# A decode kernel at full DMA: last V chunk in two transfers, output tiles ahead, half of the norm first, two weight blocks on ScalarE's queue

## Chip, core and metric

One core of one Trainium2 chip. The metric is the device time of one execution in microseconds (us), the median of several; the profile is one execution with the hardware profiler. "PE" is the matmul engine, "DVE" VectorE, "ACT" ScalarE, "POOL" GpSimd, "SP" SyncE, which issues most transfers.

## The reference, cut to what matters

One token for each of 8 sequences goes through two passes of the same pair of layers: grouped-query attention over a cache of 4096 keys and values, then a small mixer MLP.

```
def _A_ref(x, k_cache, v_cache, wq, wo):        # x: (8, 1, 448); caches: (8, 8, 4096, 256), bf16
    q = x @ wq                                  # 16 heads of 256
    p = softmax(q k^T / 16); o = p v
    return o @ wo
def _B_ref(x, w1, w2, w3, w4):
    ...                                         # with one token, the shifted mixer adds nothing
    return x1 + gelu(layernorm(x1) @ w3) @ w4
x = x + A(layernorm(x)); x = x + B(layernorm(x)); x = x + A(layernorm(x)); x = x + B(layernorm(x))
```

K and V are far larger than the on-chip memory, and the second attention needs the result of the first, so most of the caches is read twice: the trace counts 446.8 MB of reads, nearly all in chunks of 1 MB. The on-chip memory has 128 rows, called partitions; a "half block" below is a transfer that fills 64 of them.

## The kernel before

Fifteen places of 1 MB take chunks of K and V in turn; SP issues a load as soon as a place is free. While they stream, each K chunk is transposed on DVE and multiplied on PE, each V chunk multiplied on PE. Layer B of the last four sequences follows the last V chunk, so it is alone at the end. The parts that the change touches (cuts are marked `...`):

```
def load_split(t, src, cols):                   # wq (cols 4096) and w3 (cols 1792), 448 rows
    for fc in range(3):                         # three full blocks of 128 rows
        nc.sync.dma_start(t[:, fc * cols : (fc + 1) * cols], src[fc * 128 : fc * 128 + 128, :])
    nc.sync.dma_start(t[0:64, 3 * cols :], src[384:448, 0 : cols // 2])     # last 64 rows: left half
    nc.sync.dma_start(t[64:128, 3 * cols :], src[384:448, cols // 2 :])     # and right half below it
...
def norm(x, nb, twice):                         # twice: layernorm of a layernorm, two scales
    ...
    nc.vector.tensor_scalar(ve[:, 0], var, 0.0, EPS, ALU.max, ALU.add)
    if twice:
        nc.vector.tensor_scalar(ve[:, 1], var, 0.0, EPS * EPS / (1 + EPS), ALU.max, ALU.add)
    rs = room("rs", (1, 2), 560)[:, 0]
    nc.gpsimd.tensor_tensor(rs[...0:n], ve[...0:n], nhalf[...], ALU.pow)     # one power for both scales
    nc.vector.tensor_tensor(xc, x, bc(mv[:, 0]), ALU.subtract)
    ...                                         # xb, input of the next matmuls, uses rs[:, n - 1] only
    nc.vector.tensor_tensor(xc, xc, bc(rs[:, 0]), ALU.mult)                  # the other scale: residual
    nc.vector.tensor_add(x, x, xc)
...
    nc.sync.dma_start(dst[:], src)              # every K or V chunk, in emit_loads
...
    # after the last chunk:
    nc.vector.tensor_add(xs, xs, st["y"])       # residual of the attention
    nc.vector.tensor_copy(ident2, identb[:])    # identity for adding x in the output matmuls
    nc.vector.memset(o_row, 0.0)                # clear the output tile
    run(mlp_hidden(MID, Bn - MID))              # norm, @ w3, gelu
    ...                                         # @ w4, add x, four small stores
```

The softmax here doesn't subtract the row's maximum and nothing guards it: scores larger than these inputs give would overflow.

## Time and profile before

| what | value |
|---|---|
| three runs | 1115.7, 1116.61, 1117.74 us |
| profiled execution, span | 1110.0 us |
| DMA busy, mean rate over the span | full until the last slice, 404 GB/s |
| PE, DVE busy | 60%, 53% |
| last V chunk lands | 1095.86 us, 14.14 us before the end |

The lines that carry this stand in the prediction. The profiled span is shorter than the timed median because the time includes start and end around the instructions, some 1.8 us in this run (1111.84 against 1110.0), and because runs of one kernel differ by several us.

### The profile page before, as it was taken

The numbers are of one execution on the slowest core, as the hardware profiler recorded it, in microseconds if no ns is written. First come the engines' busy times: TensorE is split into PE (matmuls) and PEld (weight loads), VectorE is DVE, ScalarE is ACT, GpSimd is POOL, SyncE is SP. The second block draws the span as 40 slices with busy tenths as digits, with TensorE's granted clock in tenths as the row PEclk, the third lists the DMA queues.
The fourth block names the chain that finished last, engine by engine and source line by source line (L and its number), as shares of the span: only waits on it lengthen the run. The fifth ranks groups of instructions, "written<-read, shape, count | busy, mean of one in ns | idle before, by whom it ended". The sixth has DMA issues, their size and how long they took to land. (4 is left out here: it accounts for less than half of the span.)

```text
span 1110.0 us, 33816 instructions
## 1 busy us (share of the span) xinstructions
PE 666.6 (60%) x15606; PEld 463.1 (42%) x15606; DVE 592.6 (53%) x1010; ACT 124.6 (11%) x362; POOL 15.6 (1%) x25
## 2 busy tenths in 40 slices
PE   3135568556854578446674467844676467767775
PEld 2123345334542355324452245523454345535454
DVE  5145554646365555556465464655638463675362
ACT  0001001110110111100020000200111101111010
POOL 0000000000000000000000000000000000000000
PEclk9999999655575555555575555555557555565565
DMA  9999999999999999999999999999999999999994
GB/s 357 384 421 419 418 389 421 420 409 403 417 418 421 395 407 418 419 421 397 396 422 420 420 399 409 420 420 415 404 418 420 415 407 416 419 417 396 409 416 166
DMA packets 65181, 448.96 MB, mean 404 GB/s; under 512 B 6920, under 2 KB 10896, under 8 KB 11408
## 3 DMA queue, kind: packets, MB, share of 16 engines
q1 hardware_dynamic: 65008, 446.80, 98.4%
q8 instruction: 122, 2.00, 0.7%
q14 instruction: 19, 0.16, 0.0%
q10 hardware_dynamic: 32, 0.00, 0.0%
HBM read 446.77 MB, written 0.01 MB: 403 GB/s over the span
## 5 line engine op out<-in xcount | busy, mean ns | idle before, releaser
L632 DVE STREAM_TRANSPOSE places<-places 128x1024 uint32<-128x1024 uint32 x400 | 469.4, 1219 | 277.8 <-DMA places<-in_A_k_cache_dram 275.3
L647 PE MATMUL sc<-places,qbd 128*8 128x128 bf16 (+1 forms) x7072 | 270.2, 306 | 292.6 <-DVE places L632 250.1
L647 PEld LDWEIGHTS <-qbd 128*8 128x8 bf16 x7072 | 171.1, 106 | 366.6 <-issue 181.5
L702 PE MATMUL o<-places,ptw 128*8 128x256 bf16 x3968 | 246.1, 392 | 102.8 <-DMA places<-in_A_v_cache_dram 86.9
L656 ACT ACTIVATE p_n<-sc 128x256 bf16<-128x256 f32 x128 | 95.9, 749 | 833.6 <-PE sc L647 833.6
L702 PEld LDWEIGHTS <-ptw 128*8 128x8 bf16 x3968 | 114.2, 111 | 150.1 <-issue 108.1
L337 PEld LDWEIGHTS <-wo_sb 128*128 128x128 bf16 x1280 | 38.7, 103 | 22.9 <-issue 22.7
L284 PEld LDWEIGHTS <-wq_sb 128*128 128x128 bf16 x1152 | 35.6, 104 | 25.8 <-issue 19.0
L310 DVE TENSOR_SCALAR qbd<-misc,quad 128x64 bf16<-128x64 f32 x64 | 13.7, 277 | 52.7 <-PE misc L304 52.7
L284 PE MATMUL misc<-xb,wq_sb 128*128 128x1 bf16 x1024 | 34.4, 166 | 4.7 <-ACT ptw L690 2.8
L337 PE MATMUL misc<-OT,wo_sb 128*128 128x1 bf16 x1024 | 34.8, 165 | 2.3 <-issue 2.3
L656 ACT ACTIVATION_READ_ACCUMULATOR p_n<-sc 128x1 f32 x128 | 34.2, 267 | 0.0
L441 PEld LDWEIGHTS misc<-R,o_sb 128*128 128x128 f32 x124 | 27.3, 305 | 10.2 <-issue 9.4
L690 ACT CAST ptw<-misc 128x128 bf16<-128x128 f32 x64 | 17.5, 273 | 118.4 <-PE misc L683 63.6
L441 PE MATMUL misc<-R,o_sb 128*128 128x8 f32 x124 | 30.0, 352 | 0.2
L241 POOL TENSOR_TENSOR t<-t,nhalf 128x2 f32<-128x2 f32 (+2 forms) x18 | 13.3, 739 | 1080.4 <-DVE t L248 1080.4
L674 DVE STREAM_TRANSPOSE places<-store 128x512 uint32<-128x512 uint32 x32 | 20.1, 684 | 11.5 <-PE sc L647 11.5
L355 PEld LDWEIGHTS <-w_sb 128*128 128x128 bf16 x560 | 17.2, 105 | 10.4 <-issue 9.2
L410 PE MATMUL misc<-zm,one 128*128 128x8 f32 (+1 forms) x66 | 18.6, 356 | 4.3 <-ACT ptw L690 2.4
L355 PE MATMUL misc<-xb,w_sb 128*128 128x1 bf16 (+1 forms) x560 | 18.6, 166 | 4.0 <-DVE xb L261 2.9
L410 PEld LDWEIGHTS misc<-zm,one 128*128 128x128 f32 x66 | 15.7, 296 | 10.9 <-issue 3.7
L667 DVE STREAM_TRANSPOSE store<-places 128x512 uint32<-128x512 uint32 x32 | 20.0, 693 | 0.5
(93 smaller groups left out, 228.2 us busy)
## 6 DMA issues: line engine op xcount, KB each, us to landing
places<-in_A_v_cache_dram SPq DMA_DIRECT2D x216, 1024.0 KB, 11.0
places<-in_A_k_cache_dram SPq DMA_DIRECT2D x200, 1024.0 KB, 11.7
wo_sb<-in_A_wo_dram SPq DMA_DIRECT2D x1, 3584.0 KB, 25.3
wq_sb<-in_A_wq_dram SPq DMA_DIRECT2D x3, 1024.0 KB, 6.9
w_sb<-in_B_w_dram SPq DMA_DIRECT2D x1, 1568.0 KB, 15.5
w_sb<-in_B_w_dram SPq DMA_DIRECT2D x3, 448.0 KB, 25.2
wq_sb<-in_A_wq_dram SPq DMA_DIRECT2D x2, 256.0 KB, 10.2
w_sb<-in_B_w_dram SPq DMA_DIRECT2D x2, 112.0 KB
```

The lines of the kernel that those rows point to most:

```text
L284: nc.tensor.matmul(q_ps[:, j * Hq + h, :], w, xbs(nb)[:, xi, :], start=(fc == 0), stop=(fc == 3),)
L337: nc.tensor.matmul(y_ps[:, fc, :], w[:, i, at : at + 128], rhs(i), start=start, stop=stop, skip_group_check=open is not None,)
L355: nc.tensor.matmul(h_ps[:, c * nb : c * nb + nb], w, xbs(nb)[:, xi, :], start=(fc == 0), stop=(fc == 3),)
L410: nc.tensor.matmul(z_ps, ones, zm[:], start=True, stop=True)
L441: nc.tensor.matmul(ot_ps[:, j], o_sb[:].rearrange("p (i j) -> p j i", j=2)[:, j], R[:], start=True, stop=True)
L632: nc.vector.transpose(w, w)
L647: nc.tensor.matmul(sc[32 * k : 32 * k + 8, 128 * x : 128 * (x + nx)], qbd[:, ep, gp].rearrange("p a h -> p (a h)"), v, start=(n == 0), sto ...
L656: nc.scalar.activation(p_sb[:, :, :, 2 * u : 2 * u + 2].rearrange("p t i x -> p x t i"), sc[:, 256 * u : 256 * u + 256].rearrange("p (x t ...
L667: nc.vector.transpose(store[n][:].bitcast(U32), slot[:].bitcast(U32)[:, 512 * n : 512 * n + 512])
L674: nc.vector.transpose(slot[:].bitcast(U32)[:, 512 * n : 512 * n + 512], store[n][:].bitcast(U32))
L690: nc.scalar.copy(ptw[:, :, :, 6:8], pt_ps.rearrange("p t k (a h) -> p a (t k) h", a=4),)
L702: nc.tensor.matmul(o_ps[32 * q : 32 * q + 8, 0:256], ptz[:, at : at + 8], v[:, y * Dh : (y + 1) * Dh], start=(begin and y < 4), stop=(y >= ...
```

## The change

Its intent: shorten the chain of dependent work after the last landing, and let the two half blocks of wq and w3 be issued by two engines. The diff, cut to its core:

```
-        nc.sync.dma_start(t[64:128, 3 * cols :], src[384:448, cols // 2 :])
+        nc.scalar.dma_start(t[64:128, 3 * cols :], src[384:448, cols // 2 :])
...
+        def power(k0, k1): nc.gpsimd.tensor_tensor(rs[:, k0:k1] ..., ve[:, k0:k1] ..., ALU.pow)
         if twice:
             nc.vector.tensor_scalar(ve[:, 1], var, ...)
+            if nb > 1:
+                power(1, 2)                      # the half that xb needs
+        nc.vector.tensor_scalar(ve[:, 0], var, ...)
+        power(0, 2 if twice and nb == 1 else 1)
...
-            nc.sync.dma_start(dst[:], src)
+            if loads:
+                nc.sync.dma_start(dst[:], src)
+            else:                                # the last chunk
+                for y in range(2):
+                    nc.sync.dma_start(dst[:, 8 * Dh * y : 8 * Dh * (y + 1)], src[:, 8 * Dh * y : ...])
...
     for idx, it in enumerate(items):
+        if idx == len(items) - 2:
+            ...                                  # ident2 copy and o_row memset, moved here from the end
```

More of the change, by code (lines that the diff above doesn't have):

```diff
@@ L236, in norm, with power @@
         n = 2 if twice else 1
-        nc.vector.tensor_scalar(ve[:, 0], var, 0.0, EPS, ALU.max, ALU.add)
+        rs = room("rs", (1, 2), 560)[:, 0]
+        def power(k0, k1):
+            nc.gpsimd.tensor_tensor(
+                rs[:, k0:k1].rearrange("p n b -> p (n b)"),
+                ve[:, k0:k1].rearrange("p n b -> p (n b)"),
+                nhalf[:].to_broadcast([128, (k1 - k0) * nb]),
+                ALU.pow,
+            )
         if twice:
             nc.vector.tensor_scalar(ve[:, 1], var, 0.0, EPS * EPS / (1 + EPS), ALU.max, ALU.add)
-        rs = room("rs", (1, 2), 560)[:, 0]
-        nc.gpsimd.tensor_tensor(
-            rs[:, 0:n].rearrange("p n b -> p (n b)"),
-            ve[:, 0:n].rearrange("p n b -> p (n b)"),
-            nhalf[:].to_broadcast([128, n * nb]),
-            ALU.pow,
-        )
+            if nb > 1:
+                power(1, 2)
+        nc.vector.tensor_scalar(ve[:, 0], var, 0.0, EPS, ALU.max, ALU.add)
+        power(0, 2 if twice and nb == 1 else 1)
         xc = room("xc", (1, 4), 576)[:, 0]
@@ L623, in emit_loads @@
                 src = rows.rearrange("(p x y) d -> x p (y d)", x=4, y=16)[c]
-            nc.sync.dma_start(dst[:], src)
+            if loads:
+                nc.sync.dma_start(dst[:], src)
+            else:
+                for y in range(2):
+                    nc.sync.dma_start(
+                        dst[:, 8 * Dh * y : 8 * Dh * (y + 1)], src[:, 8 * Dh * y : 8 * Dh * (y + 1)]
+                    )
             n += 1
@@ L775 @@
     for idx, it in enumerate(items):
+        if idx == len(items) - 2:
+            end = [slots[p] for p in places[:2]]
+            ident2 = end[0][:, 0:256].bitcast(FP32)
+            nc.vector.tensor_copy(ident2, identb[:])
+            W = D // 4
+            o_row = store[0][:, 0:W]
+            nc.vector.memset(o_row, 0.0)
         n, kv, c = it
@@ L882 @@
         step(10 * len(items))
-    end = [slots[p] for p in places[:2]]
     xs = xT[:, :, MID:]
     nc.vector.tensor_add(xs, xs, st["y"])
-    ident2 = end[0][:, 0:256].bitcast(FP32)
-    nc.vector.tensor_copy(ident2, identb[:])
-    W = D // 4
-    o_row = store[0][:, 0:W]
-    nc.vector.memset(o_row, 0.0)
     run(mlp_hidden(MID, Bn - MID))
```

## The prediction

> **What bounds the kernel now.** I read the page first. Its slice rows say the transfers bound the kernel from the first slice to the last but one: in these 40 slices of 27.75 us a digit is the busy share of the 16 DMA engines in tenths, and below it stands what they moved.
>
> ```profile
> PE   3135568556854578446674467844676467767775
> DVE  5145554646365555556465464655638463675362
> DMA  9999999999999999999999999999999999999994
> GB/s 357 384 421 419 418 389 421 420 409 403 417 418 421 395 407 418 419 421 397 396 422 420 420 399 409 420 420 415 404 418 420 415 407 416 419 417 396 409 416 166
> ```
>
> No compute engine is full, DMA is full until the last slice. So 446.8 MB of reads set the time, and only two stretches can be shortened: the **head**, where the transfers start, and the **tail**, from the last landing to the end. Everything between is bytes that the change leaves alone. I then read the chain of waits that ended last (start, duration, what), cut to the tail:
>
> ```profile
> 1075.93 19.93 DMA places<-in_A_v_cache_dram
> 1095.86 0.05 issue
> 1095.91 1.03 PE store L716 x32
> ...
> 1097.82 0.17 DVE xT L887
> 1097.99 0.14 DVE places L889
> 1098.12 0.02 issue
> 1098.14 0.15 DVE store L892
> ...
> 1100.37 0.02 POOLq L241
> 1100.39 0.07 issue
> 1100.45 1.68 POOLq L948
> 1102.14 0.02 issue
> 1102.16 0.18 DVE xb L261
> ```
>
> The last V chunk lands at 1095.86 and the span ends at 1110.0: 14.1 us of tail, one instruction after another. In it are the four things the change touches: 32 matmuls behind one landing (1.03 us), the two DVE set-up instructions L889 and L892 between the residual add L887 and the norm, and 1.68 us in which DVE waits for GpSimd's power. The same chain shows nothing of the head, so I asked for the DMA activity of the first 15 us and for windows there (last column GB/s, before it the DMA share):
>
> ```profile
> GB/s 0 0 0 0 19 175 87 175 284 393 415 415 481 393 371 437 415 481 393 393 481 415 459 371 415 459 426 306 262 240 219 240 295 262 306 371 393 415 415 437
> 7.00:10.00 3.00, 0.20 (x2) 0.10 (x1) 0.51 (x3) 0.00 (x0) 1.39 (x1) 1.00 1.01 426
> 10.00:13.00 3.00, 0.19 (x1) 0.10 (x1) 0.00 (x0) 0.00 (x0) 0.00 (x0) 1.00 1.05 268
> ```
>
> A slice of the first row is 0.375 us. There is a ramp up to about 3.4 us, then full rate, then a hole of some 3 us at about 10 to 13 us where the engines are busy (1.05) but move 268 GB/s: those are the two half blocks of wq, each of 64 partitions.
>
> **What the Trainium skill says.** "SBUF — State Buffer", section on the DMA port swizzle: partitions 0 to 63 reach only the eight even ports, 64 to 127 only the eight odd ones, so a 64-partition transfer gets half the bandwidth. The trace agrees: down to 219 to 262 GB/s in the hole, against 426 just before. "DMA: Bandwidth & Descriptors", section "Issuing engines are not separate DMA queues": transfers of ScalarE and SyncE run on the same 16 engines, and a second issuer saves issue time only. The trace before has no second issuer under load, so it cannot confirm this. "GPSIMD Engine Reference", section 3.1, gives about 2.6 cycles per element for a two-input operation. Our power is far dearer by the rows below, and the rows decide.
>
> **The change part by part.**
>
> *1. Last V chunk in two transfers (tail).* The transfers of 1 MB come every 1.0486 MB / 423 GB/s = 2.48 us (423 GB/s in the window 1080 to 1085 us). The first half should land about 1.2 us before the second. The instruction order with waits shows that the first 16 matmuls then wait for the first half's semaphore and matmul 17 for the second's. 16 of 32 matmuls move ahead of the last landing: 1.03 / 2 = **-0.51 us**. Cost: rows of 4 KB instead of 8 KB, and one more issue. SP issues the last V at 1075.93, 20 us before it lands, so the issue is hidden. In the packet records an 8 KB packet takes 309 ns and an uncontended 4 KB one 159 ns; an engine has 8 rows, so 16 x 159 - 8 x 309 = **+0.07 us**.
>
> *2. Identity copy and clear made ahead (tail).* From the start of L887 (1097.82) to the start of the norm's first multiply L213 (1098.21 in the timeline; the chain's 1098.30 is cut to where L892 ends) are 0.39 us. A dependent DVE step of this kind comes 0.19 to 0.20 us after its predecessor (L213 at 1098.21, L214 at 1098.40). The order shows the two now between the third and the last scaling of O, in DVE's idle 4.85 us before the last landing. 0.39 - 0.20 = **-0.19 us**.
>
> *3. Norm's needed half first (tail).* The power's rows by form (count, busy us, mean ns):
>
> ```profile
> L241 POOL TENSOR_TENSOR t<-t,nhalf 128x2 f32<-128x2 f32 x8 | 5.6, 700 | 817.9 <-DVE t L248 817.9
> L241 POOL TENSOR_TENSOR t<-t,nhalf 128x1 f32<-128x1 f32 x8 | 4.4, 551 | 147.3 <-DVE t L248 147.3
> L241 POOL TENSOR_TENSOR t<-t,nhalf 128x8 f32<-128x8 f32 x2 | 3.3, 1644 | 115.3 <-DVE t L248 115.3
> ```
>
> These lie on a line: 395 + 156 x n ns (551, 707, 1643). The tail's instance has n = 8; only four columns are needed for xb, and after the change they are computed first. Estimate for n = 4: 395 + 624 = 1.02 us, against 1.64: **-0.62 us**. It also waits for one DVE operation fewer, whose end lies 0.08 us earlier (1100.27 instead of 1100.35): **-0.08 us**. The second power ends about 1.1 us after the first. Its users L272 and L273 serve the residual matmuls L899, which stand behind 1.76 us of hidden-layer matmuls, so it stays hidden. The single-token norms keep one power, and the other four-token norm (x2 of the form above) is under full DMA.
>
> Tail sum: -0.51 + 0.07 - 0.19 - 0.62 - 0.08 = **-1.33 us**.
>
> *4. Second half blocks on ScalarE's queue (head).* SP's L164 for wq takes 0.59 us to issue, and K follows at 3.86; but the queue is full from 3.4 us on, so the saved issue is worth nothing. What counts is the stream. 2 x 256 KB took about 2.6 us in the hole instead of 0.524 MB / 421 = 1.25; each half wastes some 0.65 us. ScalarE has nothing ahead of it, so its block is issued at about 0.75 us and its data starts at about 1.95 (SP's x: issued 0.74, and bytes appear 1.1 us later). So the two halves do not meet: SP's half still stands behind 3 MB of wq and still uses half the ports. ScalarE's half falls into the ramp, where the engines were idle for a part (shares 0.66 and 0.62 in 2.5 to 3.5: 0.36 us), but shares the odd ports with the first full block. Removed at 10 to 13 us: 1.3 us. Added at 2 to 4 us: between 0.4 (mostly in idle time) and 1.3 us (all at half rate). w3's half of 112 KB likewise: about 0.5 us removed at half rate near 38 us and the same added early. Estimate from these: **-0.4 us**, anywhere from +0.2 to -1.0. As DMA stays full to 1092 us I let it pass through to the end whole.
>
> Sum: -1.33 - 0.4 = -1.7 us; 1116.6 - 1.7 = **1114.9 us**.
>
> **The rivals.**
> - *The tail's gain is swallowed by another wait.* For: the 0.95 us issue gap of PE in the timeline near 1072 us[...]; in the tail it could sit between the halves. DVE could also wait for GpSimd at L272 into L373. Against: L273 would be done about 0.5 us before L373 is due. It would leave half of the tail's gain, 1115.7.
> - *The head gives nothing or costs.* Two rows of queues interleave on the same engines, and the odd ports are oversubscribed while the first full block runs; wq completes no earlier. Then only the tail counts: 1115.3, or 1115.6 with +0.2.
> - *The head gives all.* The ramp hides ScalarE's blocks completely: -1.3 - 0.5, total -3.1, 1113.5.
> - *A stage between eats the head's gain.* The slices at 389 to 399 GB/s show short dry spells where buffers come free late; a shift of the loads alone would be lost there. Against: computing there waits for loads too, so it shifts along.
>
> **Range and chances.** The parts spread the time from 1113.5 to 1115.7. The three runs before span 1115.7 to 1117.7, so a median can be off by about 1 us, and the profiled run of 1111.84 shows that single runs fall lower still. I widen to 1112.4 to 1116.9. A 2% step would be 22 us; the tail is 14 us in all, so faster by 2% is out of reach, and nothing added could cost 22 us but a broken wait. Chances: faster 0.01, same 0.98, slower 0.01.
>
> **What would show each step right or wrong.** In the chain: 16 matmuls L728 after the last landing, about 0.5 us; the residual add followed directly by L213; GpSimd's power at about 1.0 us with form 128x4; tail from last landing to end about 12.8 us. In the first 15 us: bytes of a second queue before 4 us and a hole at 10 to 13 us half as long; the time at which full rate is back, compared with before, gives the head's gain. It would be wrong if a 128x4 power took as long as 128x8, if the halves landed together, or if the last landing moved by more than 1 us either way.

## The result

| | before | after |
|---|---|---|
| median of 6 runs | 1116.8 us (1112.75 to 1118.64) | 1114.81 us (1111.04 to 1116.36) |
| ratio after / before | | 0.9982, 95% interval 0.9960 to 1.0004 |
| second set: median of 11 and 6 runs | 1115.6 us (1108.58 to 1120.37) | 1114.55 us (1112.31 to 1116.11) |
| ratio after / before, second set | | 0.9988, 0.9955 to 1.0021 |
| profiled span | 1110.0 us | 1109.1 us |
| last landing to the end | 14.14 us | 12.85 us |
| first V matmul (everything loaded ahead of it is in) | 48.91 us | 49.08 us |
| first 6 MB in (packet records) | 18.27 us | 19.00 us |

A ratio is the mean time of one kernel's fast runs over that of the other's of the same rounds, so not quite the ratio of the medians. Both intervals contain 1: the timed runs alone say "the same within 0.5%". What the change did has to be read from the traces.

The chain of waits of the changed kernel from the last landing on, cut (start, duration, what):

```profile
1078.88 17.37 DMA places<-in_A_v_cache_dram
1096.25 0.05 issue
1096.30 0.60 PE store L728 x16
1096.89 0.02 issue
...
1097.78 0.18 DVE xT L905
1097.96 0.02 issue
1097.98 0.18 DVE t L213
...
1100.07 0.07 DVE t L251
1100.13 0.09 DVE t L254
1100.22 1.01 POOL t L240
1101.24 0.02 issue
1101.26 0.18 DVE xb L267
```

Sixteen matmuls instead of 32 stand behind the last landing, the residual add (L905) is followed at once by the norm's first step (L213), and GpSimd's power takes 1.01 us instead of 1.68 us. The row of the power by form, which before was one of 128x8 at 1644 ns:

```profile
L240 POOL TENSOR_TENSOR t<-t,nhalf 128x4 f32<-128x4 f32 x4 | 4.0, 1012 | 114.2 <-DVE t L254 114.2
```

And the DMA activity of the first 15 us of the changed kernel: busy tenths and GB/s in 40 slices of 0.375 us, then the queues (q1 is SyncE's, q10 ScalarE's), then the windows 7 to 10 and 10 to 13 us with the GB/s at the end:

```profile
DMA  0000095589998999999999999999988999959998
GB/s 0 0 0 0 19 109 98 175 229 361 273 284 328 393 415 415 378 384 382 298 296 359 415 415 393 393 437 459 459 371 371 437 361 262 229 120 295 328 371 371
...
q1 hardware_dynamic: 600, 4.01, 76.1%
q10 hardware_dynamic: 160, 0.38, 11.6%
```

```profile
7.00:10.00 3.00, 0.17 (x1) 0.11 (x1) 0.51 (x3) 0.00 (x0) 1.38 (x1) 1.00 0.98 369
10.00:13.00 3.00, 0.19 (x1) 0.10 (x1) 0.00 (x0) 0.00 (x0) 0.00 (x0) 1.00 1.08 375
```

The window from 10 to 13 us moves 375 GB/s instead of 268, but the hole has not gone. SyncE's remaining half block now comes later (12.00 to 13.93 us by the packet records), and there the row falls to 120 GB/s: the hole is shorter (four slices under 320 GB/s instead of eight) and deeper. And there is a loss before it. Full rate is reached later (415 GB/s first in slice 15, before in slice 11), and a new dip to about 297 GB/s has come up at 7 to 8 us. The first 15 us moved 4.38 MB in all; before, 4.69 MB.

### The profile page after: what moved, and what is told of

It reads as the page before. It is cut to its first block, busy times and chain, and to the rows that moved or that the text cites. A ratio compares the mean times of both kernels' runs of the same rounds, so it can differ in the third digit from the quotient of the medians.

```text
span 1109.1 us, 33822 instructions
## 1 busy us (share of the span) xinstructions
PE 664.3 (60%) x15606; PEld 461.3 (42%) x15606; DVE 592.7 (53%) x1010; ACT 124.2 (11%) x362; POOL 16.3 (1%) x27
## 5 line engine op out<-in xcount | busy, mean ns | idle before, releaser
L714 PE MATMUL o<-places,ptw 128*8 128x256 bf16 x3968 | 243.2, 389 | 104.6 <-DMA places<-in_A_v_cache_dram 89.4
```

The lines of the kernel that those rows point to most:

```text
L714: nc.tensor.matmul(o_ps[32 * q : 32 * q + 8, 0:256], ptz[:, at : at + 8], v[:, y * Dh : (y + 1) * Dh], start=(begin and y < 4), stop=(y >= ...
```

## The experiments

My theory after the result: the tail gives about 1.3 us for sure, and the head, where I had expected 0.4 us more, gives nothing or costs some tenths. The main rival: the timed 2.0 us is real, so the head gives 0.7 us. Each trace gives two measures: **the tail** (last landing to the end), and **the first V matmul** in the timeline, which waits for a V chunk that lies in the queue behind x, the weights and the first K chunks. It is a clock of the head, but a rough one: for one and the same head it differs by up to 1.4 us (meet and best, below). The packet records have a finer one, **the first 6 MB**: the time at which SyncE's and ScalarE's queues together had moved that much, the bytes of a packet spread evenly over its time. It repeats within 0.2 us in the four traces with SyncE's order. From the same count comes the time for the 2 MB **from 3 to 5 MB**, in which the hole lies. The chips were not always the same ones.

All fourteen traces in one table ("first full" is the first packet of 8 KB that SyncE's queue moved, from the trace's packet records):

| kernel | tail us | first full us | first 6 MB us | 3 to 5 MB us | first V us | last landing us |
|---|---|---|---|---|---|---|
| before | 14.14 | 2.18 | 18.27 | 5.93 | 48.91 | 1095.86 |
| changed | 12.85 | 3.35 | 19.00 | 5.70 | 49.08 | 1096.25 |
| tail_only | 12.95 | 2.17 | 18.38 | 5.97 | 49.24 | 1099.45 |
| scalar_only | 14.07 | 3.32 | 19.65 | 6.02 | 50.04 | 1099.24 |
| meet | 14.03 | 3.99 | 18.15 | 4.71 | 48.52 | 1102.97 |
| first_sp | 14.17 | 4.36 | 18.93 | 4.69 | 50.48 | 1106.64 |
| split_only | 13.80 | 2.17 | 18.46 | 5.98 | 49.39 | 1104.20 |
| norm_only | 13.43 | 2.16 | 18.31 | 5.94 | 49.01 | 1100.36 |
| ahead_scalar | 13.92 | 3.29 | 19.73 | 6.05 | 50.03 | 1104.38 |
| scalar_late | 14.10 | 2.16 | 19.30 | 6.32 | 50.12 | 1102.40 |
| after_again (the changed kernel) | 12.89 | 3.17 | 19.87 | 6.19 | 50.29 | 1097.61 |
| scalar_wq | 14.13 | 3.12 | 18.49 | 5.73 | 48.98 | 1100.77 |
| best | 12.74 | 4.11 | 18.37 | 4.70 | 49.91 | 1099.16 |
| best_wq | 12.79 | 3.25 | 19.48 | 6.17 | 50.30 | 1096.61 |

The tail repeats to about 0.1 us; the spans in it are read to 0.1 us. The last landing spreads over 11 us although between 60 and 1060 us these kernels do the same but for two clamps in another order and one split power; the timed runs of one kernel spread as widely (1108.58 to 1120.37 us for the kernel before in one set), and so the intervals are 0.2 to 0.4% wide to each side.

Two things can be read off the table. Moving a half block to ScalarE's queue made the head slower: the six traces with wq's block in front on ScalarE had 6 MB in at 18.49 to 19.87 us (mean 19.37), the four with SyncE's order at 18.27 to 18.46 us (mean 18.35), so every one was later, by 1.0 us on average. And the hole did not cost less for it: from 3 to 5 MB took 5.93 to 5.98 us in those four, with both half blocks there, 5.70 to 6.19 us (mean 5.98) in the six with one, and 4.69 to 4.71 us in the three kernels with none there (meet, first_sp, best). One half block alone cost 1.0 to 1.5 us, as much as two in a row (1.2 to 1.3 us). Why is not shown.

### tail_only: the changed kernel without ScalarE's queue

```
-        nc.scalar.dma_start(t[64:128, 3 * cols :], src[384:448, cols // 2 :])
+        nc.sync.dma_start(t[64:128, 3 * cols :], src[384:448, cols // 2 :])
```

> The changed kernel with all half blocks back on SyncE's queue. Theory (the change's whole gain is in the tail, its head costs a little): last landing to the end of the span about 12.85 us as in the changed kernel (14.14 before); the first V matmul starts at 48.9 us as before, not at 49.1; time 1.3 to 1.5 us under the kernel before. Rival (the head gives about 0.7 us of the 2.0 us that the timed runs show): time only 1.3 us under before and clearly behind the changed kernel.

Median 1113.82 us of 6 against 1114.92 us of 11, ratio 0.999 (0.9962 to 1.0018). Tail 12.95 us, first V 49.24 us. The tail is the changed kernel's; the first V did not come at 48.9 us as expected, but the first 6 MB were in at 18.38 us, near the 18.27 us before. On time it cannot be told from the changed kernel.

### scalar_only: only the half blocks moved

```
-        nc.sync.dma_start(t[64:128, 3 * cols :], src[384:448, cols // 2 :])      # kernel before
+        nc.scalar.dma_start(t[64:128, 3 * cols :], src[384:448, cols // 2 :])
```

> The kernel before with only the two half blocks on ScalarE's queue. Theory (ScalarE's block takes the ramp, SyncE's first full block starts 1.2 us later): first 8 KB packets near 3.5 us, first V matmul at 49.1 us (48.91 before), tail 14.1 us, time within 0.5 us of before, no gain. Rival (the head gains in truth): first V matmul at 48.5 us or earlier, time about 0.7 us under before.

Median 1114.65 us, ratio 0.9995 (0.9959 to 1.0031); tail 14.07 us; first full packet 3.32 us; first V 50.04 us, 1.1 us later than before and 0.9 us later than my theory had it. The rival's 48.5 us did not come. The DMA activity of its first 15 us:

```profile
DMA  0000195939988899979999998999998999999689
GB/s 0 0 0 0 19 87 197 186 98 317 360 153 218 328 393 415 546 287 356 320 363 369 359 350 350 393 415 415 481 415 371 415 393 404 197 208 175 153 240 306
```

There is the same late ramp, the same loss at 6 to 9 us, and at the end of the row the half block left on SyncE at 153 to 208 GB/s, slower than the pair of them in the kernel before (219 to 262 GB/s).

### meet and first_sp: both half blocks of wq first, on two queues and on one

```
+    first = cols == HD                                       # wq only; w3 as before
+    if first:
+        nc.sync.dma_start(t[0:64, 3 * cols :], src[384:448, 0 : cols // 2])
+        nc.scalar.dma_start(t[64:128, 3 * cols :], src[384:448, cols // 2 :])   # first_sp: nc.sync
     for fc in range(3): ...                                  # then the three full blocks
+    if not first: ...                                        # the half blocks of w3, both on SyncE
```

> The kernel before, but the two half blocks of wq go first: the first half on SyncE right after x, the second at the same moment on ScalarE. Theory (a transfer from a second queue runs after or before the other by order of issue, they hardly mix): the halves run one after the other at half rate, some 2.5 us under 260 GB/s in the first 5 us; first V matmul near 48.9 us. Rival (the two queues mix by packets, so the halves use all ports together): both halves are in within about 1.3 us of full rate after the ramp, and the first V matmul starts 1 us or more earlier, at 47.9 us or before.

> As meet, but both half blocks on SyncE's queue: the control for the second queue. Theory (halves at half rate one after the other, partly hidden in the ramp): hole gone from 10 to 13 us, slow stretch at 2 to 5 us instead, first V matmul at 48.3 to 48.9 us. If meet is earlier than this by 0.6 us or more, the second queue lets the halves share the ports; if equal, it does not.

By the packet records both halves were moved between 2.08 and 4.74 us in meet (2.66 us) and between 2.50 and 5.38 us in first_sp (2.88 us). Neither is near the 1.25 us that the halves would take at 421 GB/s, so by the packets the second queue did not let them share all ports to any great extent, though their packets did overlap for 0.7 us (2.95 to 3.63 us). Meet's first V at 48.52 us was the best of all, first_sp's at 50.48 us the worst and far from the 48.3 to 48.9 us expected. By the measure set beforehand (0.6 us or more between them) the halves would share the ports, and the first 6 MB were in 0.78 us earlier in meet too; but 0.38 us of that was there when the first 0.1 MB was in (2.72 against 3.10 us). With one look each this stays open, and "best" below did not repeat meet's first V. Against the old head neither gained clearly: 18.15 and 18.93 us for 6 MB, against 18.35. What both did was to take the hole out; meet's first 15 us have one slice under 320 GB/s from the sixteenth on:

```profile
GB/s 0 0 0 0 19 87 164 284 317 262 197 197 240 197 328 350 306 371 371 568 393 371 371 371 568 415 371 371 415 524 415 371 371 459 502 415 350 393 481 481
```

### split_only, norm_only, ahead_scalar: the tail's parts alone

Each is the kernel before with one part of the diff above; ahead_scalar also has the half blocks on ScalarE, as a further trace of that head.

> The kernel before with only the last V chunk in two transfers. Theory (the three tail parts add up): 16 matmuls after the last landing taking 0.55 to 0.6 us, tail from last landing to the end about 13.7 us (14.03 to 14.16 in four traces with the old tail). Rival (the tail parts overlap, the split gives nothing alone because PE's weights wait anyway): 14.1 us. First V matmul at 48.9 to 49.3 us, as the two traces with this head have it.

> The kernel before with only the needed half of the norm first. Theory: from the start of the variance's first clamp to the start of xb 1.37 us (2.06 before), tail 13.4 us. Rival (the second power on GpSimd holds up DVE's later work): xb early, but the hidden layer's first DVE step no earlier, tail 14.1 us. First V matmul at 48.9 to 49.3 us.

> The kernel before with the output tiles made ahead and the half blocks on ScalarE's queue: a third trace of this head, and the tiles alone in the tail. Theory: the norm's first multiply starts 0.20 us after the residual add (0.39 before), tail 13.9 us; SyncE's first 8 KB bytes again near 3.5 us and the first V matmul at 49.0 to 50.1 us, never before 48.9. Rival (the head gains): first V matmul at 48.5 us or earlier.

Old tails: 14.03 to 14.17 us in six traces, mean 14.11. Split_only 13.80 (-0.31), norm_only 13.43 (-0.68), ahead_scalar 13.92 (-0.19): together -1.18 us, and the three kernels with all parts as in the change have 12.85, 12.95 and 12.89, mean 12.90 (-1.21). The parts add up. (Split_only's matmuls saved more, 0.42 us: its residual add starts 1.54 us after the landing, 1.96 us in the kernel before. The missing 0.1 us lies behind xb, 7.91 us to the end against 7.81, where the two kernels are alike.) In split_only's timeline one sees the first half at work while the second is on its way:

```profile
1103.01 0.59 PE L722 MATMUL store<-ptw,places 128*128 128x2 bf16 x16 [0.23 <-DMA places<-in_A_v_cache_dram]
1104.25 0.51 PEld L722 LDWEIGHTS <-places 128*128 128x128 bf16 x16 [0.74 <-DMA places<-in_A_v_cache_dram]
1104.25 0.59 PE L722 MATMUL store<-ptw,places 128*128 128x2 bf16 x16 [0.66 <-DMA places<-in_A_v_cache_dram]
```

The halves come 1.24 us apart, and 0.59 us of matmuls stand behind the last. In norm_only's timeline the second power is hidden:

```profile
1104.92 2.00 POOL L240 TENSOR_TENSOR t<-t,nhalf 128x4 f32<-128x4 f32 x2 [70.02 <-DVE t L254]
1105.97 0.55 DVE L267 SCALAR_TENSOR_TENSOR xb<-t 128x12 bf16<-128x12 f32 x3 [1.05 <-POOL t L240]
1106.95 0.18 DVE L278 TENSOR_TENSOR t<-t 128x16 f32<-128x16 f32 x1 [0.42 <-POOL t L240]
```

POOL works 2.00 us on both powers, but xb starts after the first, at 1105.97. DVE waits 0.42 us for the second before the residual scale (L278), while PE is at the hidden layer. From the variance's first clamp (1104.60) to xb are 1.37 us, as against 2.06 before (1100.10 to 1102.16).

Ahead_scalar's norm starts 0.21 us after the residual add (1106.33 to 1106.54), as expected. Its head: first full packet 3.29 us, first V 50.03 us.

### scalar_late: ScalarE's block issued after SyncE's blocks

```
     nc.vector.tensor_copy(xT[:], ps0)
+    nc.scalar.copy(late[:], xT[:, 0, 0:1])                   # makes ScalarE wait for xT
+    nc.scalar.dma_start(wq_sb[64:128, 3 * HD :], A_wq[384:448, HD // 2 :])   # no longer in load_split
```

> The kernel before with wq's second half block alone on ScalarE's queue, issued only after xT is copied, near 4.5 us, when SyncE has issued all its blocks of wq. Theory of turns (engines alternate between the two queues by whole transfers): its bytes come within about 3 us of its issue, between two full blocks, and SyncE's first full block starts near 2.4 us again. Rival theory of order (one line for both queues by time of issue): its bytes come only after SyncE's half block and a K chunk, after 11 us. If the late block beside full traffic costs no more than alone, first V matmul at 48.9 to 49.3 us.

ScalarE issued it at 4.48 us. Its packets ran from 8.27 to 11.10 us, so 3.8 us after the issue, later than "within 3 us". But they ran ahead of SyncE's own half block, which had been issued two microseconds earlier (2.53 us) and ran from 11.51 us. One line by time of issue is refuted; the engines took the second queue's transfer between SyncE's blocks. SyncE's first full packet came at 2.16 us again, so what delays it in the change is ScalarE's block in front of it. The late block was no free ride either: first V 50.12 us. The windows 8 to 13 us of scalar_late, then of the kernel before, with GB/s at the end:

```profile
8.00:13.00 5.00, 0.19 (x2) 0.10 (x1) 0.51 (x3) 0.00 (x0) 0.40 (x1) 1.00 1.04 309
```

```profile
8.00:13.00 5.00, 0.38 (x3) 0.21 (x2) 0.51 (x3) 0.00 (x0) 0.39 (x1) 1.00 1.03 329
```

Busy engines, and still fewer bytes than with both half blocks in one row. The 3 MB from 2 to 5 MB took 9.21 us, against 8.28 to 8.38 us with the two in a row and 7.08 to 7.11 us with none there: apart, the two half blocks cost 2.1 us, in a row 1.2 to 1.3 us. Whether it is the half blocks or the full blocks beside them that were slowed is not shown.

### after_again, scalar_wq, best, best_wq

After_again is the changed kernel unaltered. Scalar_wq moves wq's half block alone to ScalarE. Best has the tail parts with the last chunk in four transfers and meet's head; best_wq has the same tail and scalar_wq's head.

```
-                for y in range(2):                            # best, best_wq, on the changed kernel
-                    nc.sync.dma_start(dst[:, 8 * Dh * y : 8 * Dh * (y + 1)], ...)
+                for y in range(4):
+                    nc.sync.dma_start(dst[:, 4 * Dh * y : 4 * Dh * (y + 1)], ...)
...
+        (nc.scalar if cols == HD else nc.sync).dma_start(t[64:128, 3 * cols :], ...)  # scalar_wq (on the kernel before), best_wq
```

> The changed kernel once more. Theory (tail -1.3 us for sure, head +0.2 to +0.9 us): tail 12.85 to 12.95 us, first 8 KB bytes of SyncE near 3.5 us, first V matmul at 49.1 to 50.0 us, time 0.4 to 1.1 us under before, ratio 0.999 to 1.000. Rival (head neutral or better): first V matmul below 49.0 us, ratio 0.998 again.

> The kernel before with only wq's second half block on ScalarE's queue, w3's stays on SyncE. Theory A (wq's block, first through the ramp, makes the cost): first 8 KB bytes near 3.5 us and first V matmul at 49.6 to 50.0 us. Theory B (w3's block, mixed with wq's full blocks at 6.4 to 8.8 us, makes the cost): first 8 KB bytes near 3.5 us but first V matmul at 48.3 to 49.1 us.

> A version meant to beat both: the three tail parts, the last V chunk in four transfers instead of two, and wq's two half blocks first, one on each queue, with w3 wholly on SyncE. Theory: 8 matmuls after the last landing instead of 16, so tail 12.6 us; head as in meet, first V matmul at 48.3 to 48.8 us (49.14 mean of four traces of the old head); time 1.9 to 2.2 us under before, ratio 0.998. Rival (the one look at meet was chance): first V matmul at 48.9 us or later, time 1.5 us under.

> The three tail parts with the last V chunk in four transfers, and only wq's second half block on ScalarE's queue, w3 wholly on SyncE: a second look at the head of scalar_wq. Theory (w3's block among the full blocks makes the cost of the changed head): tail 12.6 to 12.8 us, first V matmul at 48.9 to 49.4 us, time 1.0 to 1.5 us under before, ratio 0.999. Rival (the 48.98 us of scalar_wq was chance, wq's block costs too): first V matmul at 49.8 us or later.

After_again: tail 12.89 us, first V 50.29 us, past the upper end of what I expected. The rival's early first V has come in no trace of this head.

Scalar_wq's 48.98 us spoke for w3's block as the cause of the head's cost, but best_wq, with the same head, had 50.30 us, so that theory fell as the whole cause. In part it holds: the 2 MB from 1 to 3 MB took 5.18 to 5.25 us in the four traces with w3's block on ScalarE, 4.73 and 4.74 us in these two and 4.69 to 4.80 us with SyncE's order, so w3's block costs about 0.5 us, and wq's the rest. What the six traces with ScalarE's wq block in front do show is two groups. By the packet records ScalarE's block took 1.90 and 1.85 us in the changed kernel's trace and scalar_wq, and there the first V came at 49.08 and 48.98 us; it took 2.26 to 2.37 us in scalar_only, ahead_scalar, after_again and best_wq, and there the first V came at 50.03 to 50.30 us. The two go together six times of six, and the first 6 MB do so too (19.00 and 18.49 us against 19.48 to 19.87); why the block is quick or slow at the start I could not settle.

Best failed in its head: first V 49.91 us, not 48.3 to 48.8; meet's early one had been chance or needs something else. By the first 6 MB (18.15 and 18.37 us) this head is about as good as SyncE's order, and not better. Its tail is 12.74 us and best_wq's 12.79: eight matmuls after the last landing (here best_wq's chain) are worth some 0.13 us more than sixteen.

```profile
1096.61 0.05 issue
1096.66 0.39 PE store L728 x8
```

Best timed 1114.7 us against 1115.6, ratio 0.9991 (0.9957 to 1.0025). Best_wq timed 1112.43 us against 1115.56, ratio 0.9988 (0.9961 to 1.0014). None is shown to beat the changed kernel. The version that the traces would recommend, the tail with four transfers and all half blocks on SyncE, was not run as a whole. Nor was a full block on ScalarE's queue tried, which would tell what a second queue costs from what a lone half block costs.

## Why the prediction was right, and where not

The time (1114.81 against 1114.9 us) and the class were right. The steps:

1. **What bounds the kernel**: right. DMA is full in both traces to the last slice but one, and only head and tail moved.
2. **Last chunk in two**: expected -0.51 + 0.07. The matmuls behind the landing went from 1.03 to 0.60 us (-0.43), because 16 matmuls take somewhat more than half of 32; split_only's tail showed -0.31. The rest of the difference lies in a stretch that the split does not touch. The 0.07 us would delay the last landing and so is not in the tail as measured. Right in mechanism, a little too large.
3. **Tiles ahead**: expected -0.19; from residual add to the norm's first step 0.39 us became 0.20, and ahead_scalar's tail was 0.19 shorter. Right.
4. **Needed half first**: expected -0.62 and -0.08. The line 395 + 156 x n gave 1.02 us for n = 4 and 1.01 was measured; with the earlier start -0.69 in the chain, -0.68 in norm_only's tail. Right, and the second power stayed hidden as argued.
5. **Tail sum**: -1.33 expected (-1.40 without the 0.07 us that lies before the landing), -1.21 measured over three and six traces. Right.
6. **ScalarE's queue**: wrong, and two terms of its sum failed. The first is "each half wastes some 0.65 us", by which one half less in the hole would save that much. The loss there did not change: 1.28 us on average in six traces with one half block, 1.2 to 1.3 us in four with two. The half block that stayed wasted 1.0 to 1.5 us by itself. The prediction had split the pair's loss evenly, and the trace before the change shows no lone one. The second is "ScalarE's half falls into the ramp, where the engines were idle for a part". Its bytes did flow before 4 us, but they did not fill gaps: they ran in front, and SyncE's first full packet came at 3.12 to 3.35 us in six traces instead of 2.16 to 2.18 in five. The first 1 MB was in at 5.65 to 6.19 us instead of 5.23 to 5.34, on average 0.7 us later. That is the upper end of the range given: 1.3 us ("all at half rate") less the 0.6 us that its bytes need anyway. w3's block lost 0.5 us more. Instead of -0.4 us, the first 6 MB were in 1.0 us later on average, and the first V matmul came 0.65 us later (49.79 in six traces against 49.14 in four, whose ranges overlap). The sign set for this step, a hole half as long, came true all the same: the hole was shorter and deeper, and its length alone did not measure the loss.
7. **"I let it pass through to the end whole"**: right as far as it can be followed. The delay of 1.0 us is still there when 50 MB are in (126.3 to 127.5 us in the six traces, 126.0 to 126.2 in the four). At 100 MB the traces spread too widely (248.7 to 251.3 and 248.5 to 249.6), and the last landing varies by 11 us over the same middle: it was as early as 1096.25 and 1096.61 us with ScalarE's queue and 1095.86 us without.

Of the rivals, "the head gives nothing or costs" was the one that came, and it cost more than its +0.2; the tail was not swallowed by another wait. That the median still met the predicted one to 0.1 us is luck: the traces make -1.21 + 1.0, so about -0.2 us, if the head passes on to the end, and not -1.7; the two timed sets gave -0.18% and -0.12% with half-widths of 0.22% and 0.33%, too wide to tell these apart.

## What to carry to other kernels

When one resource is full from start to end, work on the chain after its last byte: there every dependent step counts, it can be added up from the trace in advance, and it repeats to a tenth of a microsecond when the whole time does not. Cut the last transfer so that only a part of its work stands behind it, move setup ahead of it, and compute first what the next engine waits for. A second issuing queue is no free lane: put nothing inefficient in front of the stream on it, and measure its effect near the start, by the time at which a fixed number of bytes is in, rather than at the end. A loss that two transfers make together need not halve when one of them is moved away.

## What the Trainium skill lacked or had wrong

- "GPSIMD Engine Reference", section 3.1, has about 2.6 cycles per element for a two-input add and nothing for a power. Here a power of 128 x n elements took 551, 700, 1012 and 1644 ns for n = 1, 2, 4 and 8, about 395 + 156 x n.
- "DMA: Bandwidth & Descriptors", "Issuing engines are not separate DMA queues", says that a second issuer saves the sequencer's time only. The runs agree that it brought no bandwidth (6 MB were in 1.0 us later on average), but it also changes the order: ScalarE's block of 256 KB, issued 0.44 us before SyncE's first full block, held that back by 1.0 to 1.2 us in six traces.
- The same page, "Queues, rings and completion order", has the engines go round-robin between queues by packet. Scalar_late agrees in kind: the later-issued block of the other queue overtook a block of SyncE's issued two microseconds earlier (8.27 against 11.51 us). It waited 3.8 us from issue to first byte behind a full stream, for which the page has no figure.
- "SBUF — State Buffer", the DMA port swizzle: agrees for two 64-partition blocks in a row (219 to 262 GB/s); a lone one among full blocks ran slower (153 to 208 GB/s in scalar_only). Its section "Can I just issue two DMAs to hit both halves?" says that two transfers cannot be fused; meet, with the two halves on two queues at once, moved them in 2.66 us against 2.88 us on one queue, which agrees, with one look each. None of the pages read has what a lone half-port block costs among full ones: 1.0 to 1.5 us here, as much as two in a row (1.2 to 1.3 us), where half the rate for its 0.262 MB would make about 0.6 us (an estimate from 0.262 MB at 421 GB/s).
- None of the pages read has how much executions of one DMA-bound kernel differ: here 1108.6 to 1120.4 us for the kernel before in one set.
